# A two-layer MLP behind a short convolution: two more of the second layer's Strassen products split once more

## The chip, the cores and the metric

The kernel runs on one core of a Trainium2 chip. The metric is the time of one execution on the device in microseconds (us), as the median of several runs.

## The reference

`x` is (8, 4096, 192), 32,768 tokens of 192 values. A causal convolution over 7 tokens weighs each channel by a softmax over its head's 7 taps; the result goes through an MLP, 192 to 2048 with a hardswish gate and back to 192. All is float32.

```python
w = softmax(weight, axis=-1)                          # (8 heads, 7 taps)
y = np.einsum('hk,bskhg->bshg', w, x_unf)             # x_unf: 7 shifted views of padded x
h = y.reshape(32768, 192) @ w_in                      # 192 -> 2048
g = h * np.clip(h + 3.0, 0.0, 6.0) / 6.0
out = g @ w_out                                       # 2048 -> 192
```

## The kernel before, in words

The tokens are cut into 32 blocks of 1024 (`TB`), each two groups of N = 512. The two groups lie on the two halves of the 128 partitions, so a copy with the halves swapped (`swap_parts`) serves the other group. Block 0 has a path of its own (`out_direct`) that runs while weights are prepared. Blocks 1 to 31 run `first_layer` and then `second_layer`. All is under `tc.manual_schedule()`: each engine executes its instructions in the order in which the code issues them, and a block's first and second layers follow each other on TensorE.

**First layer.** y and w_in are split into three parts each (HIGH, LOW, MIX), and each of 16 steps n runs 18 matmuls (L508) into one PSUM slot of two banks. ACT multiplies the slot by 4097 between the parts (L520) and makes the relu (L302); VectorE makes the gate (L306), which writes g and releases the slot. Four slots rotate. Steps 0 to 7 give the quarters A11 and A22 of g, steps 8 to 15 give A21 and A12. Beside these steps GpSimd forms small sums of A11 (L578) and the sum S3 = A11 - A21 (L412, `g_sums`), and starts DMAs that add A22 onto A21 in place (L557, S1 = A21 + A22). The last two pairs of S1 are added by VectorE (L559). The convolution of a later block (L919, L921) is placed between as `jobs`.

**Second layer.** The contraction over 2048 with 192 outputs is a 2x2 matrix product by Strassen, with seven products P1 to P7 (`prod`), each over eight chunks of 128, 512 tokens wide and 96 output rows. The rows are three quarters of 32, and TensorE runs four column streams side by side, stream j writing rows 32j to 32j+31 of a PSUM bank. A plain step is a matmul of 512 columns; `put` counts it as 2 units, a small one of 256 columns as 1. Streams 0 to 2 run the three quarters of P4, P7, P2, P6 and P3. Stream 3 runs the first two quarters of P1 and of P5 by Strassen once more (`level_two`, seven small products of four 256-column matmuls), and their third quarter as plain steps: 82 units on each stream.

The small products need small weights (`w_s`, formed once, L587) and small sums of their operand: `s1` (of A11, on GpSimd) and `s5` (of S1, in A22's place, on VectorE, L578). Their results are passed between places in PSUM by ACT copies (L695 to L701) and VectorE adds (L456).

The order around the change is set by hand. `put` and `do` collect closures with a time in units, `do(t, ...)` at t - 0.5, and `second_layer` sorts all of them by time and runs them; that gives every engine's queue. `between` brings in the next block's split of y (L474, L937, L477), the swap, the load of x and some taps of the convolution. PSUM slots come from `free_slots`: the slots of gates 12, 13 and 14 become the banks d, e; b, x_; a, c. Two final sums and stores (`finish`) are left over and run as `jobs[-1]` of the next block's first layer. In the last block `ends`, `end_lower` and `end_upper` store in pieces.

Of the kernel before, what the change touches and what calls it, by code (L numbers as in the profile page):

```python
# [25 lines left out]
def kernel(  # L26
# [93 lines left out]
    w_s = cst.tile([P, 2, 4, NP // 2, QS], F32, name="w_s")  # L120
# [245 lines left out]

    new_results()
# [34 lines left out]
    def g_sums(engine, which, slots, width):  # L402

        forms = {
            3: (S3, A11, A21, ALU.subtract),
            2: (S2, S1, A11, ALU.subtract), 4: (S3, A12, S2, ALU.subtract),
        }
        for n in which:
            o, a, b, op = forms[n]
            for p in slots[::width]:  # L410
                r = slice(p, p + width)
                engine.tensor_tensor(out=o[:, r], in0=a[:, r], in1=b[:, r], op=op)  # L412
# [75 lines left out]
    y_own, y_other, pools, s1 = [], [None], [], []  # L488

    def swap_parts():  # L490
        y_other[0] = pools[0].tile([P, 3, K3, N], F32, name="y_other", tag="other")
        for n in range(3):
            swap(y_other[0][:, n], y_own[n])


    def first_layer(i, jobs):
# [6 lines left out]
        def mms(n, part, start=False, stop=False):  # L503
            group, c = divmod(n, NP)
            for s in range(K3):
                for k in range(2):
                    r = slice(k * D2, (k + 1) * D2)
                    nc.tensor.matmul(  # L508
                        out=psum[:, 2 * slots[n] + k], lhsT=r32(w_in_parts[part][r, c, s]),
                        rhs=r32(y_other[0][r, part, s] if group else y_own[part][r, s]),  # L510
                        start=start and s == 0, stop=stop and s == K3 - 1,
                        skip_group_check=True,
                    )
# [27 lines left out]
        for n in range(count):  # L541
# [7 lines left out]
            if n == 1:  # L549
                s1.append(ot.tile([P, NP, N], F32, name="s1", tag="shared")[:])  # L550
            if n < NP and n % 2:
                small_sums(s1[-1], A11, (1, 2, 3, 4), nc.gpsimd, every[n - 1 : n + 1])
            if n > NP and n % 2:
                pair = slice(n - NP - 1, n - NP + 1)
                g_sums(nc.gpsimd if n + 1 < count else nc.vector, (3,), range(NP)[pair], 2)
                if n + 3 < count:
                    nc.gpsimd.dma_start(out=S1[:, pair], in_=A22[:, pair], accum_op=ALU.add)  # L557
        for pair in (slice(NP - 2, NP), slice(NP - 4, NP - 2)):
            add(S1[:, pair], A21[:, pair], A22[:, pair])  # L559
# [20 lines left out]
    def small_weights(to, w):  # L580

        b11, b12, b21, b22 = (
            w_out[:, c::2, w, q * QS : (q + 1) * QS] for c in range(2) for q in range(2)
        )
        t1, t2, t3, t4 = (to[:, n] for n in range(4))
        for o, p, q in ((t1, b12, b11), (t2, b22, t1), (t3, b22, b12), (t4, b21, t2)):
            nc.gpsimd.tensor_tensor(out=o, in0=p, in1=q, op=ALU.subtract)  # L587

    def second_layer(i, between):
# [3 lines left out]
        ends = [psum[:, 2 * free_slots[0] + k] for k in range(2)] if last else [b, b]  # L593
        s5 = A22
        copy = nc.scalar.copy
        m = slice(0, DH)
        lo, hi = halves
        both = nc.sync, nc.scalar
        B, C, V = (bank[rows(3)] for bank in (x_, d, b))
        A, E = e[rows(3)], a[rows(3)]  # L600
        first, second, third, fourth = (rows(q) for q in range(4))
        late = {}
# [17 lines left out]
        def plain(j, bank, n, q, chunks, start=False):  # L620
            x, w = prod[n]
            x = S3 if x is None else x
            for k, ch in enumerate(chunks):
                put(j, 2, lambda ch=ch, k=k: matmul(
                    j, bank[rows(j)], w_out[:, ch, w, q * QS : (q + 1) * QS], x[:, ch],
                    start and k == 0,
                ))

        def small(n, m_, out, start=False):

            x, w = prod[n]
            sums, ws = (s1[-1], w_s[:, 0]) if n == 1 else (s5, w_s[:, 1])
            x11, x12, x21, x22 = four_parts(x)
            z1, z2, z3, z4 = four_parts(sums)
            b11, b12, b21, b22 = (
                w_out[:, h::2, w, q * QS : (q + 1) * QS] for h in range(2) for q in range(2)
            )
            t1, t2, t3, t4 = (ws[:, k] for k in range(4))
            xm, wm = {
                1: (x11, b11), 2: (x12, b21), 3: (z4, b22), 4: (x22, t4),  # L640
                5: (z1, t1), 6: (z2, t2), 7: (z3, t3),
            }[m_]
            for u in range(NP // 2):
                put(3, 1, lambda u=u: matmul(
                    3, out[:, lo], wm[:, u], xm[:, u], start and u == 0
                ))

        def plain_by_halves(j, n, q, t):
            w = prod[n][1]
            for ch in every:  # L650
                put(j, 1, lambda ch=ch: matmul(
                    j, ends[t][rows(j), halves[t]], w_out[:, ch, w, q * QS : (q + 1) * QS],
                    S3[:, ch, halves[t]], ch == 0,
                ))

        def tiles():
            new_results()
            if last:
                xts.insert(0, NP - 1)
            late.update(zip(("p7", "p5", "u3"), (results[0][m, n] for n in range(3))))  # L660

        for q in range(NQ):
            plain(q, d, 4, q, every, True)
            before = (1, 6, NP)[q]
            plain(q, c, 7, q, every[:before], True)
            plain(q, e, 1, 2, range(5 + q, 6 + q))
            do(clock[q], copy, out=e[rows(q + 1)] if q < 2 else p1[third], in_=e[rows(q)])
            plain(q, c, 7, q, every[before:])
            plain(q, a, 2, q, every[:6], True)
            plain(q, b, 6, q, every)  # L670
            plain(q, a, 2, q, every[6:])
            if last:
                plain_by_halves(q, 3, q, 0)
                plain_by_halves(q, 3, q, 1)
            else:
                plain(q, b, 3, q, every)

        def level_two(n, p, chunks, order):
            chunks, first_fill = list(chunks), [True]
            left = [list(chunks) for _ in halves]  # L680

            def fill_half(t, k):
                for _ in range(k):
                    ch = left[t].pop(0)
                    x, w = prod[n]
                    put(3, 1, lambda ch=ch: matmul(
                        3, (ends[0], x_)[t][fourth, halves[t]], w_out[:, ch, w, 2 * QS : 3 * QS],
                        x[:, ch, halves[t]], ch == 0,
                    ))

            def fill(k):
                plain(3, b, n, 2, [chunks.pop(0) for _ in range(k)], first_fill.pop() if first_fill else False)

            steps = {
                1: lambda: copy(out=B[:, lo], in_=A[:, lo]),  # L695
                2: lambda: copy(out=p()[first, lo], in_=A[:, lo]),
                6: lambda: copy(out=C[:, lo], in_=B[:, lo]),
                5: lambda: copy(out=p()[second, lo], in_=E[:, lo]),
                7: lambda: add(p()[second, hi], C[:, lo], p()[second, lo]),
                3: lambda: add(p()[second, lo], B[:, lo], p()[second, lo]),  # L700
                4: lambda: copy(out=p()[first, hi], in_=C[:, lo]),  # L701
            }
            to = {1: A, 2: A, 6: B, 5: E, 7: C, 3: B, 4: C}
            for step in order.split():
                if step[0] == "x":
                    fill(int(step[1]))
                elif step[0] in "lh":
                    fill_half("lh".index(step[0]), int(step[1]))
                else:
                    k = int(step)  # L710
                    small(n, k, to[k], k in (1, 5))
                    do(clock[3], steps[k])

        level_two(1, lambda: p1, range(5), "1 x5 6 5 2 7 3 4")
        do(14, copy, out=e[first], in_=V)
        level_two(
            5, lambda: late["p5"], range(NP),
            "1 l4 2 6 5 7 3 l2 4 l2 h8" if last else "1 x2 2 6 5 7 3 x1 4 x5",
        )

        for t, job in between:
            do(t, job)
        for t, n in ((16.2, 1), (16.2, 2), (30.5, 3), (34.5, 4)):
            do(t, small_sums, s5, S1, (n,), nc.vector)
        do(32, tiles)
        do(34, lambda: copy(out=late["p7"], in_=c[m]))
        do(38, copy, out=b[m], in_=p1[:])
        do(38, g_sums, nc.vector, (2,), every, 4)
        do(38, g_sums, nc.vector, (4,), every, 4)
        do(62, lambda: add(late["u3"], b[m], late["p7"]))  # L730
        do(62, lambda: add(late["p7"], late["u3"], d[m]))
        do(62, lambda: store(i, late["p7"], 1, 0))
        do(66, add, p1[:], a[m], p1[:])
        do(66, lambda: store(i, p1, 0, 0))

        def finish(k):
            p5, u3 = late["p5"], late["u3"]
# [6 lines left out]
        def end_lower():  # L744
            p5, u3, c12 = late["p5"], late["u3"], results[0][m, 6]
            two = slice(0, 2 * QS)
# [272 lines left out]
```

## Time and profile before

| what | value |
|---|---|
| median of 3 runs (lowest, highest) | 2226.74 us (2226.70, 2226.88) |
| span of the profiled execution | 2224.9 us |
| TensorE matmul busy | 2218.0 us |
| VectorE (DVE) busy | 1894.3 us |
| ScalarE (ACT) busy | 1379.2 us |
| GpSimd (POOL) busy | 823.8 us |
| one block in mid-run: first layer, second layer | 32.90 us, 35.47 us |

The profile is of one execution, whose span is 1.8 us shorter than the median of the runs. In its rows, `L615 PE MATMUL psum<-g,w_out 128*32 128x512 f32 x5440` is line 615, engine, operation, what it writes and reads, the tile and how often it runs; behind the bar stand the busy time and the mean duration in ns, and behind the second bar the engine's idle time just before, with what ended it. PEld is TensorE's weight load, which runs beside its matmuls. "POOLq" and "SPq" are the queues of the engines that issue DMAs. A timeline row begins with its start and its duration in us.

### The profile page before, as it was taken

To read this page: it belongs to the slowest core of one execution; us is meant where nothing else is said; L and a number is where in the kernel's file an instruction comes from. 1 tells how busy PE (TensorE), PEld (TensorE's weight loads), DVE (VectorE), ACT (ScalarE), POOL (GpSimd) and SP (SyncE) were. 2 spreads that over 40 slices of the span, in tenths; PEclk is the share of its full clock that TensorE was granted. 3 is DMA by queue.
4 is the path that set the end of the run, shared out by engine and by line. 5 is a ranking of instruction groups with operands and counts; after the bars stand their busy time and mean duration, and the time that the engine had idled before them with its cause. 6 is when DMAs were issued, how large, how long until landed. Compare 5 with 4: busy or idle time off the path is not lost.

```text
span 2224.9 us, 50339 instructions
## 1 busy us (share of the span) xinstructions
PE 2218.0 (100%) x21496; PEld 1532.7 (69%) x21496; DVE 1894.3 (85%) x1673; ACT 1379.2 (62%) x1678; POOL 823.8 (37%) x690
## 2 busy tenths in 40 slices
PE   9999999999999999999999999999999999999999
PEld 5467776677766777766777667776677776677766
DVE  8888888888888888888888888888888888888876
ACT  7457665576655676555766557665567655576654
POOL 2344432344422444223443234442244422344323
PEclk9999999999999999999999999999999999999999
DMA  6244224443244342344422444324434234442232
GB/s 157 57 98 85 49 58 91 85 83 62 53 82 91 77 80 47 71 91 84 85 48 58 91 87 81 67 49 82 91 79 81 47 67 91 84 84 52 55 77 34
DMA packets 253584, 166.57 MB, mean 75 GB/s; under 512 B 208017, under 2 KB 213137, under 8 KB 253361
## 3 DMA queue, kind: packets, MB, share of 16 engines
q1 hardware_dynamic: 234872, 129.46, 28.4%
q0 software_dynamic: 17248, 33.64, 8.7%
q8 instruction: 168, 2.75, 0.5%
q14 instruction: 56, 0.45, 0.1%
q10 hardware_dynamic: 1240, 0.27, 0.1%
HBM read 31.72 MB, written 25.17 MB: 26 GB/s over the span
## 4 chain that ended last, share of the span: by engine, by line
PE 99%; DVE 0%; DMA 0%; ACTq 0%; issue 0%; DVEq 0%; ACT 0%
PE psum L615 49%; PE psum L508 46%; PE psum L296 2%; PE psum L341 2%; DMA x<-in_x_dram 0%; DVE y L255 0%; DVE top L175 0%; ACTq L89 0%; PE psum L816 0%; DVE results L456 0%; DVE scale L171 0%; DVE y L251 0%; DVE scale L192 0%; DVEq L1014 0%; DVE results L462 0%
## 5 line engine op out<-in xcount | busy, mean ns | idle before, releaser
L615 PE MATMUL psum<-g,w_out 128*32 128x512 f32 (+1 forms) x6712 | 967.5, 552 | 0.0
L306 DVE SCALAR_TENSOR_TENSOR g<-g,psum 128x1024 f32<-128x1024 f32 (+1 forms) x528 | 618.3, 1186 | 198.8 <-ACT g L302 194.5
L578 POOL TENSOR_TENSOR s<-g 128x256 f32<-128x256 f32 x248 | 273.6, 1103 | 1241.1 <-DVE g L306 1200.5
L302 ACT ACTIVATE g<-psum,half 128x1024 f32<-128x1024 f32 (+1 forms) x528 | 564.8, 1087 | 6.0 <-PE psum L508 5.2
L615 PEld LDWEIGHTS psum<-g,w_out 128*32 128x32 f32 x6712 | 371.8, 110 | 246.0 <-issue 126.7
L508 PE MATMUL psum<-y,w_in 64*128 64x512 f32 x4464 | 521.4, 388 | 0.0
L508 PE MATMUL psum<-y_other,w_in 64*128 64x512 f32 x4464 | 516.0, 386 | 0.0
L520 ACT ACTIVATE psum<-psum 128x1024 f32<-128x1024 f32 x465 | 469.0, 1008 | 50.7 <-PE psum L508 48.4
L508 PEld LDWEIGHTS psum<-y,w_in 64*128 64x128 f32 x4464 | 413.5, 184 | 115.7 <-issue 26.0
L508 PEld LDWEIGHTS psum<-y_other,w_in 64*128 64x128 f32 x4464 | 418.1, 184 | 87.8
L615 PE MATMUL psum<-s,w_out 128*32 128x512 f32 (+1 forms) x3272 | 465.5, 570 | 0.0
L921 DVE SCALAR_TENSOR_TENSOR y<-x,c_sb,y 128x1536 f32<-128x1536 f32 x186 | 335.2, 1802 | 2.6 <-ACT y L919 1.3
L412 POOL TENSOR_TENSOR s<-g 128x1024 f32<-128x1024 f32 x93 | 285.9, 3074 | 26.2 <-DVE g L306 26.2
L615 PE MATMUL psum<-g,w_s 128*32 128x256 f32 x1240 | 282.8, 379 | 0.0
L615 PEld LDWEIGHTS psum<-s,w_out 128*32 128x32 f32 x3272 | 154.3, 110 | 81.9 <-issue 49.4
L615 PEld LDWEIGHTS psum<-g,w_s 128*32 128x32 f32 x1240 | 136.4, 110 | 67.7
L412 DVE TENSOR_TENSOR s<-g 128x2048 f32<-128x2048 f32 (+1 forms) x93 | 181.3, 1977 | 1.1
L615 PE MATMUL psum<-s,w_s 128*32 128x256 f32 x744 | 170.7, 379 | 0.0
L578 DVE TENSOR_TENSOR g<-g 128x1024 f32<-128x1024 f32 x124 | 151.7, 1224 | 5.3
L412 DVE TENSOR_TENSOR g<-g 128x2048 f32<-128x2048 f32 x62 | 139.1, 2284 | 0.0
L612 ACT COPY psum<-psum 32x512 f32<-32x512 f32 x93 | 51.3, 551 | 135.4 <-PE psum L615 135.4
L456 DVE TENSOR_TENSOR results<-psum,results 32x256 f32<-32x256 f32 (+3 forms) x128 | 69.3, 541 | 50.9 <-issue 45.5
(91 smaller groups left out, 1299.5 us busy)
## 6 DMA issues: line engine op xcount, KB each, us to landing
y_other<-y SPq DMA_DIRECT2D x186, 384.0 KB, 5.1
g<-g POOLq DMA_DIRECT2D x62, 512.0 KB, 5.0
out_dram<-results SPq DMA_DIRECT2D x378, 64.0 KB, 2.0
x<-in_x_dram SPq DMA_DIRECT2D x53, 388.5 KB, 7.7
stage<-in_moe_w_in_dram SPq DMA_DIRECT2D x16, 192.0 KB, 4.5
stage<-in_moe_w_out_dram SPq DMA_DIRECT2D x8, 384.0 KB, 6.8
x<-in_x_dram SPq DMA_DIRECT2D x7, 384.0 KB, 8.4
x<-in_x_dram POOLq DMA_DIRECT2D x2, 388.5 KB, 5.4
```

What stands on the lines that cost most here:

```text
L296: nc.tensor.matmul(out=psum[:, b], lhsT=w[r], rhs=src, start=start, stop=stop, skip_group_check=onto,)
L302: nc.scalar.activation(r6, h, ACT.Relu, bias=half[:], scale=1.0 / 6.0)
L306: nc.vector.scalar_tensor_tensor(out=g_, in0=g_, scalar=1.0, in1=h, op0=ALU.min, op1=ALU.mult)
L341: lambda p=p: nc.tensor.matmul(out=bank[j * QS : (j + 1) * QS, tokens], lhsT=w_out[:, p, w, cols], rhs=x[:, p, tokens], start=(first and p ...
L412: engine.tensor_tensor(out=o[:, r], in0=a[:, r], in1=b[:, r], op=op)
L456: nc.vector.tensor_tensor(out=out, in0=x, in1=y, op=op)
L508: nc.tensor.matmul(out=psum[:, 2 * slots[n] + k], lhsT=r32(w_in_parts[part][r, c, s]), rhs=r32(y_other[0][r, part, s] if group else y_own[ ...
L520: nc.scalar.mul(both(n), both(n), 4097.0)
L578: engine.tensor_tensor(out=o, in0=p, in1=q, op=op)
L612: streams[3].append((t - 0.5, lambda: fn(*args, **kw)))
L615: nc.tensor.matmul(out=out, lhsT=w, rhs=x, start=start, stop=True, tile_position=(0, j * QS), skip_group_check=True,)
L921: jobs.append(lambda k=k: nc.vector.scalar_tensor_tensor(out=y[:], in0=x[:, :, k : k + N], scalar=c_sb[:, k : k + 1], in1=y[:], op0=ALU.mu ...
```

## The change

P4 and P7 too go by Strassen once more, as P1 and P5 do, and the streams are laid out anew: 80 units each.

- Stream 0: P2's first quarter, the third quarters of P1 and P5, then P6 and P3. Stream 1: P2's second quarter, the seven small products of P4 with one of P5's in a place of its own (`aside`), P6, P3. Stream 2: P2's third quarter, the third quarters of P4 and P7, P6, P3. Stream 3: the small products of P1, P7 and P5.
- The sums for P4 (of A22) are formed by DMA: four copies on SyncE's queue after step 7 of the first layer (`copy_for_sums`), then four adding DMAs from GpSimd's queue behind steps 9, 11 and 13 (`add_for_sums`), into y's own region (`sums4`).
- S1 is formed wholly by adding DMAs, four in place of two and two VectorE adds. S3's sum for n = 13 moves from GpSimd to VectorE.
- The sums for P7 (of S3) are formed on VectorE in the region of `y_other` (`sums7`); those for P5 (of S1) by four ACT multiplies by 1 or -1 and four adding DMAs (`sums_by_dma`).
- P4's sums have the other sign (`PLUS`), so one quarter of its weights is negated once by ACT, and its steps negate and subtract.
- Split of y, swap and load of x move later in the second layer; results lie in A22; the last block loses its own tail.

The core of the diff:

```diff
         for n in range(count):
...
             if n < NP and n % 2:
-                small_sums(s1[-1], A11, (1, 2, 3, 4), nc.gpsimd, every[n - 1 : n + 1])
+                small_sums(sums[1], A11, (1, 2, 3, 4), nc.gpsimd, every[n - 1 : n + 1])
+            if n == NP - 1:
+                sums[4] = sums_in("own", "sums4")
+                copy_for_sums(sums[4], A22)
             if n > NP and n % 2:
                 pair = slice(n - NP - 1, n - NP + 1)
-                g_sums(nc.gpsimd if n + 1 < count else nc.vector, (3,), range(NP)[pair], 2)
-                if n + 3 < count:
-                    nc.gpsimd.dma_start(out=S1[:, pair], in_=A22[:, pair], accum_op=ALU.add)
-        for pair in (slice(NP - 2, NP), slice(NP - 4, NP - 2)):
-            add(S1[:, pair], A21[:, pair], A22[:, pair])
+                early = n + 3 < count
+                if n in ADD_AHEAD:
+                    add_for_sums(sums[4], A22, ADD_AHEAD[n])
+                g_sums(nc.gpsimd if early else nc.vector, (3,), range(NP)[pair], 2)
+                nc.gpsimd.dma_start(out=S1[:, pair], in_=A22[:, pair], accum_op=ALU.add)
+                if n in ADD_BEHIND:
+                    add_for_sums(sums[4], A22, ADD_BEHIND[n])
+
+    ADD_AHEAD = {NP + 1: (1,), NP + 3: (2,)}
+    ADD_BEHIND = {NP + 3: (3,), NP + 5: (4,)}
...
+    def copy_for_sums(to, x):
+        x11, x12, x21, x22 = four_parts(x)
+        s1, s2, s3, s4 = four_parts(to)
+        for o, p in ((s1, x22), (s2, x11), (s3, x11), (s4, x12)):
+            nc.sync.dma_start(out=o, in_=p)
+
+    def add_for_sums(to, x, which):
...
+        forms = {1: (s1, x21), 2: (s2, s1), 3: (s3, x21), 4: (s4, s2)}
+        for n in which:
+            o, p = forms[n]
+            nc.gpsimd.dma_start(out=o, in_=p, accum_op=ALU.add)
+
+    def sums_by_dma(to, x, n):
...
+        o, p, scale, q = {
+            1: (s1, x22, 1.0, x21), 2: (s2, x11, -1.0, s1),
+            3: (s3, x21, -1.0, x11), 4: (s4, s2, -1.0, x12),
+        }[n]
+        nc.scalar.mul(o, p, scale)
+        nc.gpsimd.dma_start(out=o, in_=q, accum_op=ALU.add)
...
+    def small_weights(n):
+        b11, b12, b21, b22 = w_quarters(n)
+        t1, t2, t3, t4 = w_smalls(n)
+        third = (t3, b12, b22) if n == PLUS else (t3, b22, b12)
+        for o, p, q in (third, (t1, b12, b11), (t2, b22, t1), (t4, b21, t2)):
             nc.gpsimd.tensor_tensor(out=o, in0=p, in1=q, op=ALU.subtract)
+        if n == PLUS:
+            nc.scalar.mul(b22, b22, -1.0)
...
+        s3_places = e[fourth, lo], a[fourth, lo], x_[fourth, lo], d[fourth, lo]
+        s1_places = e[second, lo], c[second, lo], x_[second, lo], x_[second, hi]
+        aside = c[second, hi]
+        places = {1: s3_places, 4: s1_places, 5: s3_places, 7: s3_places}
+        onto = {1: b, 4: d, 5: p5, 7: p7}
...
+        def step(n, k):
+            A, E, B, C = places[n]
+            p, plus = onto[n], n == PLUS
+            op = ALU.subtract if plus else ALU.add
+            if k == 1:
+                (negated if plus else copy)(out=B, in_=A)
+            elif k == 2:
+                copy(out=p[first, lo], in_=A)
+            elif k == 6:
+                copy(out=C, in_=B)
+            elif k == 5:
+                (negated if plus else copy)(out=stash(n), in_=E)
+            elif k == 7:
+                add(p[second, hi], C, stash(n), op)
+            elif k == 3 and plus:
+                add(p[second, lo], stash(n), B, op)
+            elif k == 3:
+                add(p[second, lo], B, stash(n))
+            else:
+                copy(out=p[first, hi], in_=C)
...
         for q in range(NQ):
-            plain(q, d, 4, q, every, True)
...
+            plain(q, a, 2, q, True)
+        plain(0, e, 1, 2, True)
+        do(clock[0], copy, out=b[third], in_=e[first])
+        plain(0, x_, 5, 2, True)
+        do(clock[0] + 1, copy, out=p5[third], in_=x_[first])
+        for k in (1, 5, 6, 2, 7, 3):
+            small(1, 4, k)
+            do(clock[1], step, 4, k)
+        small(1, 5, 4, aside)
+        small(1, 4, 4)
+        do(clock[1], step, 4, 4)
+        do(clock[1] + 1, copy, out=p5[first, hi], in_=aside)
+        plain(2, d, 4, 2, True)
+        plain(2, c, 7, 2, True)
+        do(clock[2] + 1, copy, out=p7[third], in_=c[third])
+        for q in range(NQ):
+            plain(q, b, 6, q)
+            plain(q, b, 3, q)
+
+        waiting = {(7, 5): 48.5, (7, 2): 48.6, (7, 7): 49}
+        for n, k in (
+            [(1, k) for k in (1, 5, 6, 2, 7, 3)] + [(7, 1), (1, 4)]
+            + [(7, k) for k in (5, 6, 2, 7, 3)] + [(5, 1), (7, 4)]
+            + [(5, k) for k in (5, 6, 2, 7, 3)]
+        ):
+            small(3, n, k)
+            do(waiting.get((n, k), clock[3]), step, n, k)
+        do(clock[3] - 4 + 0.2, lambda: add(p5[first, hi], places[5][3], p5[first, hi]))
...
+        do(0.6, sums7)
+        do(21, lambda: small_sums(sums[7], S3, (4,), nc.vector))
+        for t, n in ((30, 1), (33, 3), (37, 2), (58, 4)):
+            do(t, sums5, n)
+        do(32.4, lambda: copy(out=spare["own"][m], in_=b[m]))
+        do(32.6, lambda: add(a[m], a[m], spare["own"][m]))
+        do(33, g_sums, nc.vector, (2,), every[: NP // 2], 4)
+        do(37, g_sums, nc.vector, (2,), every[NP // 2 :], 4)
+        do(50, g_sums, nc.vector, (4,), every[: NP // 2], 4)
+        do(53, g_sums, nc.vector, (4,), every[NP // 2 :], 4)
         for t, job in between:
             do(t, job)
...
+        do(57, lambda: store(i, a, 0, 0))
+        do(64.2, lambda: add(u3, b[m], p7))
+        do(64.3, lambda: add(p7, u3, d[m]))
+        do(64.4, lambda: store(i, p7, 1, 0))
...
             if i + 1 < NB:
-                between = [(13, split_high), (15, split_rest), (18, swap_parts)]
+                between += [(40.4, split_high), (41, split_low), (49.5, split_mix), (53, swap_parts)]
```

In the changed file the first layer's matmul is line 522, its gate 307, its multiply 534, the second layer's matmul 670, S1's adding DMA 574, the adding DMAs of P4's sums 614, of P5's sums 625 with their ACT multiply 624, the negation of weights 646, and `step` 720 to 734.

## The prediction

> **What bounds the kernel now.** I began with the page's busy shares, then its chain that ended last.
>
> ```profile
> PE 2218.0 (100%) x21496; PEld 1532.7 (69%) x21496; DVE 1894.3 (85%) x1673; ACT 1379.2 (62%) x1678; POOL 823.8 (37%) x690
> ...
> PE 99%; DVE 0%; DMA 0%; ACTq 0%; issue 0%; DVEq 0%; ACT 0%
> ```
>
> TensorE is never idle, and 99% of the chain is its own work, so only less matmul or a new wait of TensorE can change the time. The chain in order of time gives a block:
>
> ```profile
> 1057.14 32.90 PE psum L508 x288
> 1090.05 35.47 PE psum L615 x216
> ```
>
> A block is 32.90 us of first layer and 35.47 of second, 68.37 together, and 31 blocks follow. The second layer is 82 units (256 columns on each of the four streams). In the timeline the sets of stream matmuls start at 1096.44, 1096.87 and 1097.30: a unit is 0.43 us (35.47 / 82 = 0.433).
>
> Third, how a hand-over from TensorE to another engine and back looks:
>
> ```profile
> 1097.33 0.59 PE L615 MATMUL psum<-s,w_s 128*32 128x256 f32 x2
> ...
> 1097.99 0.34 ACT L697 COPY psum<-psum 32x256 f32<-32x256 f32 x1 [1.10 <-PE psum L615]
> ...
> 1098.78 0.55 ACT L612 COPY psum<-psum 32x512 f32<-32x512 f32 x1 [0.45 <-PE psum L615]
> ...
> 1099.38 0.11 PEld L615 LDWEIGHTS psum<-g,w_out 128*32 128x32 f32 x1 [0.21 <-ACT psum L612]
> ...
> 1099.49 0.59 PE L615 MATMUL psum<-g,w_out 128*32 128x256 f32 x2
> ```
>
> The set begun at 1097.33 is done a unit later, 1097.76, and ACT starts at 1097.99: 0.2 us. The L612 copy ends at 1099.33 and the weight load that waited for it runs at 1099.38: 0.05, then 0.11 for the load. So a hand-over costs 0.2 + the operation + 0.16. This load belongs to stream 3's row quarter, and the copy touches another quarter of the same PSUM bank: the program waits by bank. Such waits exist 62 times:
>
> ```profile
> PEld psum L615 <- ACT psum L612: 13.8, 62, 0.2
> ```
>
> They cost TensorE nothing: two units (0.86 us) lie between the producer matmul and the waiting one, and the hand-over takes about that.
>
> **What the change removes.** Two units of 82: 0.86 us a block, 26.6 in 31. Before's 2226.7 less that is 2200.
>
> **What it adds.** Every wait of TensorE in the changed second layer follows from its instruction order and semaphores, and many now have *no* unit between the producer and the waiter. Positions are units from the second layer's start; the steps (product, small product) are those of the code.
>
> *a) The boundary, unit 0.* P2 now comes first, in bank a, which is the PSUM slot that gate 14 of the first layer reads. Before, P4's bank d came first, free two gates earlier.
>
> ```profile
> 1089.94 3.48 DVE L306 SCALAR_TENSOR_TENSOR g<-g,psum 128x1024 f32<-128x1024 f32 x3 [1.17 <-ACT g L302]
> 1089.97 6.64 PE L615 MATMUL psum<-g,w_out 128*32 128x512 f32 x63
> 1093.45 1.71 DVE L412 TENSOR_TENSOR s<-g 128x1024 f32<-128x1024 f32 x1
> ```
>
> Those are gates 13 to 15, 1.16 us apart: gate 13 ends at 1091.10. The change also moves S3's sum for n = 13 from GpSimd into VectorE's queue just behind gate 13. So 1091.10 + 1.37 (row below) + gate 14's 1.22 + 0.16 = 1093.85 against 1089.97: **3.9 us**.
>
> *b) Hand-overs without slack.* With the copy's 0.34 to 0.37 and the add's 0.43, one costs 0.7 (ACT) or 0.8 (VectorE). They stand at units 8 (copy of (1,5)), 16 ((1,2)), 20 ((4,1) and (1,7)), 24 ((1,3) add), 28 (two copies in a row, 1.05) and 48 ((4,4)): 0.72 + 0.72 + 0.82 + 0.85 + 1.05 + 0.7 = **4.9 us**. Each stops all streams, because TensorE's queue is in order.
>
> *c) Unit 33.* The matmul of (7,5) in bank a waits for VectorE's a += P1, behind four ACT copies that follow unit 32 (0.55, 0.36, 0.36, 0.58): 0.2 + 1.85 + 0.2 + 0.69 (96x512 add) less the unit between, 0.43: **2.5 us**.
>
> *d) Units 36 and 40.* (4,7) and (4,3), VectorE adds that now release bank x_, stand behind the halves of S2's sum.
>
> ```profile
> L412 DVE TENSOR_TENSOR g<-g 128x2048 f32<-128x2048 f32 x62 | 139.1, 2284 | 0.0
> ...
> L412 DVE TENSOR_TENSOR s<-g 128x1024 f32<-128x1024 f32 x31 | 42.3, 1365 | 1.1
> ```
>
> From VectorE's free moment in c): at 36, 2.28 + 0.43 + 0.16 less 3 units = **1.5**; at 40, 2.28 + 0.43 + an ACT copy's 0.35 less 4 units = **1.3**.
>
> *e) Unit 49.* Three more ACT copies (0.37, 0.37, 0.58) less a unit: **0.9**.
>
> *f) Unit 60.* The matmul of (5,5) in bank a waits for a's transpose, behind (7,7) 0.43, the split 1.75, S4's first half 2.28, (7,3) 0.43, the second half 2.28, the transpose 0.71: 7.9 us, beside which 11 units (4.7) and e)'s stall (0.9) pass: **2.2**.
>
> *g) Unit 64.* u3 must read b before P3 is added to it: 0.69, **0.7**.
>
> Sum 3.9 + 4.9 + 2.5 + 1.5 + 1.3 + 0.9 + 2.2 + 0.7 = 17.9, less 0.86: 17.0 a block, 528 in 31.
>
> *Costed at nothing.* VectorE's adds for S3's small sums (4 x 1.22) replace S1's small sums; GpSimd's A11 sums (L578) end at +24 us, ahead of unit 4. ACT gains four 1.0-us operations (L624) in a second layer where it idles half the time; without that cover, c) grows by 1.0 each.
>
> *DMA.* A block's adding DMAs go from 2 to 12, all in GpSimd's queue, and SyncE gets four copies of 512 KB.
>
> ```profile
> g<-g POOLq DMA_DIRECT2D x62, 512.0 KB, 5.0
> ...
> q0 software_dynamic: 17248, 33.64, 8.7%
> q1 hardware_dynamic: 234872, 129.46, 28.4%
> ```
>
> 8.7% of the span over 62 accumulations bounds one at 3.1 us of all 16 engines: 12 cost up to 37 us. With the 20 that queue 1 takes in a block now (28.4% of 2224.9, over 31), and four copies (2 us each by the rate of the swaps, six of 384 KB in about 10 us), the engines would be busy some 66 of 85 us. Early use has slack: the first needed lands before unit 20. The new accumulations move rows of 1 KB, before's 2 KB, which no row shows. Bounds: same price per byte (nothing added); twice as long (12 x 3.1 more than a block holds: the sum S1 late by 5 to 10 us). I take the same price, nearest to this row; the upper end widens the range. Issues occupy GpSimd:
>
> ```profile
> L557 POOL DMA_DIRECT2D g<-g x62 | 74.5, 1201 | 19.9 <-POOL s L412 19.9
> ```
>
> Ten more are 12 us, on an engine with 60% idle: cost nothing.
>
> *Once.* In the first block ACT's negation of B22 waits for seven weight sums of GpSimd and holds the convolution's first multiply and L520 behind it.
>
> ```profile
> L587 POOL TENSOR_TENSOR w_s<-w_out 128x128 f32<-128x128 f32 x4 | 5.4, 1342 | 1.0 <-DVE w_out L212 1.0
> ```
>
> From 94.9: 7 x 1.34 = 9.4, + 0.5 + 1.6, so 106.4 against 101.5, and VectorE behind it: between 5 and 8, I take 7. The last block loses its split tail (an add, transpose and store later): 0 to 4, I take 2.
>
> The profiled execution: 2224.9 + 528 + 7 + 2 = 2761.9; around the span lie 1.8 us (median 2226.7): **2764**.
>
> **Two rules weighed.** The Trainium skill, "PSUM — Partial Sum Buffer", section "PSUM bank collisions raise a hardware error", says that two engines may touch one bank at once if they are in different quarters of 32 rows. The 0.2-us waits above show this program waiting across quarters nevertheless; by the rule only a) and g) are needed, and a program guarded so would take 2200 + 31 x 4.6 + 9 = 2352 (estimate). "TensorE: Matmul & The Clock Gate", Part 1, speaks against the change: an idle window of about 3.4 us halves the clock for as long. No idle gap lies in before's trace (clock digits 9 throughout), so none here shows it; with a) in each block it would add about 1.7 x 31 = 53 (estimate).
>
> **Rivals.**
> 1. *DMA late.* If 1-KB rows cost 1.5 times, or the queue backs up, ACT's L624 (which waits for all four S1 sums and stands ahead of c)) starts 4 to 8 us late: 31 x 4 to 8 over the forecast, 2890 to 3010. For it: slack at unit 28 of about 1 us. Against: 5.0 us to landing.
> 2. *Shorter stalls.* If ACT's and VectorE's hand-overs run partly inside the drain of the other streams, b) to f) fall by a third: 13.3 / 3 x 31 = 137 less, 2627. For it: the free 0.2-us waits.
> 3. *Faster.* The waits cost nothing as the 62 do now: it holds only if every wait lies within TensorE's buffered work, decides where stalls sum below 0.86 us a block, and gives 2200 + 9 = 2209. Against: buffered work shown covers 0.2 us; a) alone is 3.9.
> 4. *The units aren't saved*: streams of 256 columns load weights twice as often, 6 x 0.11 = 0.66 in 0.86 us; before 5. It would add 26.6: 2791. Against: the loads still fit.
>
> **Chances.** Forecast's band, 2690 to 2850, with rival 4 inside: 70%. Rival 1: 14%. Rival 2: 12%. Rival 3: 4%. The range takes in half of rivals 1 and 2: 2620 to 2940. A change under 0.2% can't be told from none in this measurement; faster by more 0.03, same 0.01, slower 0.96.
>
> **What would show it.** TensorE's busy share falls to about 80%; the first second-layer matmul waits 3 to 4 us for VectorE L307; VectorE and ACT enter the chain with about a fifth of it; the matmul work itself shrinks by 0.86 us a block. Waits of TensorE on DMA would mean rival 1; a share above 95% would make the prediction wrong.

## The result, and the profile after

The changed kernel takes 2997.65 us (median of 4 runs, 2989.08 to 3003.57) against 2226.81: 1.346 times as long, 95% interval [1.344, 1.348]. The profiled execution has a span of 2994.9 us. A block takes 93.2 us where it took 68.4: 24.8 more, and 31 times that is the whole difference of 770 us in span.

The page of the changed kernel, busy times first and then the queues:

```profile
PE 2458.3 (82%) x22920; PEld 1565.5 (52%) x22920; DVE 2002.7 (67%) x1791; ACT 1553.0 (52%) x2018; POOL 1101.0 (37%) x972
...
q0 software_dynamic: 164992, 196.12, 42.9%
q1 hardware_dynamic: 301880, 194.68, 27.3%
...
sums<-g POOLq DMA_DIRECT2D x155, 512.0 KB, 7.7
...
g<-g POOLq DMA_DIRECT2D x124, 512.0 KB, 8.5
```

TensorE is idle for 18% of the span; before it was never idle. The adding DMAs of queue 0 take 42.9% of the 16 engines' time, 8.7% before, and one needs 6.1 to 8.5 us from issue to landing (medians of the page, by what it writes and reads), 5.0 before. Both dynamic queues together are 2102 us of DMA work, 68 us of a 93-us block (26.6 before).

Who held TensorE, from the view of the waits (us in total, times, longest):

```profile
PEld psum L670 <- DVE g L307: 191.3, 31, 7.2
...
PE psum L670 <- DVE g L307: 178.2, 31, 6.7
...
PEld psum L670 <- DVE psum L462: 151.5, 93, 2.4
...
PEld psum L670 <- DMA sums<-g: 94.8, 30, 3.9
...
PEld psum L670 <- DVE g L468: 77.0, 31, 2.5
```

In each of the 31 blocks the second layer's first weight load waits 6.2 us for gate 14 (L307), and the matmuls stand idle for 5.75. Three times a block an add (L462) holds TensorE, once the transpose of a (L468), once a DMA into the small sums. The forecast had all but the last.

Where in the second layer the time goes can be read to the unit: stream 3 starts one small matmul per unit, so a start that comes later than 0.4287 us after the one before is a stall or a slow unit. The table gives the means over 31 blocks in us a block, for the forecast, the changed kernel, and some of the experiments below. The row of unit 0 has an ordinary step of 0.6 in it (all that is left of it in e2, e7, e9 and e11), and in the changed kernel 0.4 of slow clock as well (e4, at full clock, has 6.4 there).

| units | held by | forecast | changed | e2 | e3 | e5 | e7 | e9 | e11 |
|---|---|---|---|---|---|---|---|---|---|
| 0 | gate 14 (a) | 3.9 | 6.8 | 0.6 | 6.8 | 6.8 | 0.6 | 0.6 | 0.6 |
| 2 to 6 | matmuls at half clock | 0 | 1.8 | 0 | 1.3 | 2.1 | 0 | 0 | 0 |
| 8 to 28 | hand-overs (b) | 4.2 | 4.3 | 5.8 | 4.3 | 1.5 | 5.8 | 0.9 | 0 |
| 32, 34 | a += P1 (c) | 2.5 | 2.2 | 7.0 | 2.2 | 0.1 | 2.2 | 0.1 | 0 |
| 36 to 44 | VectorE, DMA (d) | 2.8 | 3.1 | 3.1 | 3.1 | 8.6 | 3.1 | 4.4 | 0.5 |
| 48 to 52 | ACT copies (b, e) | 1.6 | 1.3 | 1.3 | 1.3 | 1.3 | 1.8 | 0.4 | 0.7 |
| 60, 62 | transpose of a (f) | 2.2 | 2.2 | 2.2 | 2.2 | 0 | 2.2 | 0.1 | 0.2 |
| 64 to 70 | u3 (g) | 0.7 | 0.5 | 0.5 | 0.5 | 1.4 | 1.4 | 4.1 | 3.6 |
| 76, 78 | P5's fourth small sum | 0 | 3.3 | 2.9 | 0 | 5.2 | 0.1 | 2.4 | 0 |
| block | | 85.4 | 93.2 | 90.9 | 88.8 | 95.1 | 84.2 | 80.7 | 72.8 |

Steps b) to g) come to 14.0 in the forecast and 13.6 measured. What the forecast lacks stands in three rows: unit 0, the half clock behind it, and unit 76. The boundary, in the timeline of the changed kernel:

```profile
1434.02 1.22 DVE L307 SCALAR_TENSOR_TENSOR g<-g,psum 128x1024 f32<-128x1024 f32 x1 [1.16 <-ACT g L303]
1434.46 1.29 POOL L614 DMA_DIRECT2D sums<-sums  x1 [3.05 <-DMA sums<-g]
1435.26 2.86 POOL L418 TENSOR_TENSOR s<-g 128x1024 f32<-128x1024 f32 x1
1435.28 3.94 DVE L418 TENSOR_TENSOR s<-g 128x1024 f32<-128x1024 f32 x1
...
1439.14 2.34 DVE L307 SCALAR_TENSOR_TENSOR g<-g,psum 128x1024 f32<-128x1024 f32 x2
...
1440.40 4.41 PE L670 MATMUL psum<-g,w_out 128*32 128x512 f32 x23 [6.27 <-DVE g L307]
```

The moved sum L418 takes 3.94 us on VectorE, not 1.37: it starts with GpSimd's own L418 (the sum for n = 11) and ends 1.1 us after it, about what it takes alone. Over the 31 blocks it takes 2.26 to 4.40 us, 3.41 on average. GpSimd's is that late because its queue stood 3.05 us at L614, P4's second adding DMA, which waits for the first to land. Then 23 matmul records take 4.41 us, where 24 took 2.36 in the kernel before. The same stretch cut by time (window, its length, busy time and count of PE, PEld, DVE, ACT and POOL, granted clock, DMA share, GB/s) shows why:

```profile
1440.40:1443.80 3.40, 3.40 (x20) 1.50 (x24) 3.26 (x3) 0.00 (x0) 3.40 (x4) 0.50 1.10 173
1443.80:1447.20 3.40, 2.84 (x33) 1.29 (x29) 2.63 (x3) 0.71 (x2) 0.91 (x1) 0.88 1.17 169
1447.20:1460.00 12.80, 10.99 (x129) 5.66 (x125) 3.92 (x4) 3.15 (x7) 0.00 (x0) 1.00 0.73 121
```

The clock is 0.50 for the first 3.4 us. Over the run it is granted at half for 262 us, in pieces of 3.4, 6.8 and 10.2 us; before, for 4.7 us at the start. And unit 76:

```profile
1386.63 1.06 ACT L624 ACTIVATE sums<-sums 128x1024 f32<-128x1024 f32 x1
1387.98 1.28 POOL L625 DMA_DIRECT2D sums<-g  x1 [12.30 <-ACT g L734]
1388.01 1.58 SPq L267 DMA_DIRECT2D y_other<-y_own  x1
...
1399.31 0.40 PE L670 MATMUL psum<-sums,w_out 128*32 128x256 f32 x1 [1.87 <-DMA sums<-g]
```

P5's fourth small sum is issued at 1388.0, together with the last two swap DMAs of the next block's y, and TensorE's matmul that needs it starts 11.3 us later.

### The profile page after: what moved, and what is told of

Read it like the earlier page. It is cut to its first block, busy times and chain, and to the rows that moved or that the text cites. A ratio compares the mean times of both kernels' runs of the same rounds, so it can differ in the third digit from the quotient of the medians.

```text
span 2994.9 us, 55245 instructions
## 1 busy us (share of the span) xinstructions
PE 2458.3 (82%) x22920; PEld 1565.5 (52%) x22920; DVE 2002.7 (67%) x1791; ACT 1553.0 (52%) x2018; POOL 1101.0 (37%) x972
## 3 DMA queue, kind: packets, MB, share of 16 engines
q0 software_dynamic: 164992, 196.12, 42.9%
## 5 line engine op out<-in xcount | busy, mean ns | idle before, releaser
L670 PE MATMUL psum<-g,w_out 128*32 128x512 f32 (+1 forms) x7440 | 1244.8, 594 | 326.7 <-DVE g L307 178.2
L307 DVE SCALAR_TENSOR_TENSOR g<-g,psum 128x1024 f32<-128x1024 f32 (+1 forms) x528 | 621.8, 1186 | 203.2 <-ACT g L303 202.7
L670 PE MATMUL psum<-sums,w_out 128*32 128x256 f32 x1984 | 466.2, 404 | 199.0 <-DMA sums<-g 67.5
L522 PE MATMUL psum<-y_own,w_in 64*128 64x512 f32 x4464 | 528.4, 392 | 0.2 <-DVE results L403 0.2
L598 POOL TENSOR_TENSOR sums<-g 128x256 f32<-128x256 f32 x248 | 273.3, 1102 | 677.2 <-DVE g L307 676.5
L522 PEld LDWEIGHTS psum<-y_own,w_in 64*128 64x128 f32 x4464 | 429.5, 186 | 99.5 <-issue 18.7
L670 PE MATMUL psum<-sums,w_s 128*32 128x256 f32 x1984 | 477.4, 381 | 0.0
L670 PEld LDWEIGHTS psum<-sums,w_out 128*32 128x32 f32 x1984 | 203.2, 116 | 413.6 <-DMA sums<-g 94.8
L462 DVE TENSOR_TENSOR psum<-psum,sums 32x256 f32<-32x256 f32 (+1 forms) x124 | 62.0, 500 | 383.3 <-PE psum L670 230.0
L462 DVE TENSOR_TENSOR g<-psum,g 32x256 f32<-32x256 f32 (+1 forms) x217 | 108.7, 501 | 306.5 <-PE psum L670 218.9
L670 PE MATMUL psum<-s,w_out 128*32 128x256 f32 (+1 forms) x992 | 294.6, 489 | 0.0
L418 DVE TENSOR_TENSOR g<-g 128x2048 f32<-128x2048 f32 x124 | 283.5, 2287 | 2.0
L670 PEld LDWEIGHTS psum<-sums,w_s 128*32 128x32 f32 x1984 | 202.8, 109 | 84.9 <-DVE psum L462 26.6
L574 POOL DMA_DIRECT2D g<-g x124 | 195.9, 1580 | 18.4 <-POOL s L418 18.4
```

Source lines behind the costliest of these rows:

```text
L307: nc.vector.scalar_tensor_tensor(out=g_, in0=g_, scalar=1.0, in1=h, op0=ALU.min, op1=ALU.mult)
L462: nc.vector.tensor_tensor(out=out, in0=x, in1=y, op=op)
L522: nc.tensor.matmul(out=psum[:, 2 * slots[n] + k], lhsT=r32(w_in_parts[part][r, c, s]), rhs=r32((y_other if group else y_own)[0][r, part, s ...
L598: engine.tensor_tensor(out=o, in0=p, in1=q, op=op)
L670: nc.tensor.matmul(out=out, lhsT=w, rhs=x, start=start, stop=True, tile_position=(0, j * QS), skip_group_check=True,)
```

## The experiments

Theory A was: the excess over the forecast is these three things (VectorE's sum beside GpSimd's, the clock after idleness, the sum that lands beside the swap), and the rest are the waits by bank without slack of the forecast. Each run has one edit to the changed kernel unless it says otherwise; times are medians, beside 2226.8 for the kernel before and 2997.65 for the changed one.

**e1, S3's sum behind the gates.**

```diff
-                g_sums(nc.gpsimd if early else nc.vector, (3,), range(NP)[pair], 2)
+                if early:
+                    g_sums(nc.gpsimd, (3,), range(NP)[pair], 2)
+                elif n + 1 == count:
+                    g_sums(nc.vector, (3,), every[NP - 4 :], 2)
```

> Only S3's sum for n = 13 moves, from between gates 13 and 14 on VectorE to behind gate 15. Theory A (the 6.2-us boundary stall is the sum ahead of gate 14, 1.4 us of its own and 2.6 of standing beside GpSimd's L418): gate 14 ends about 2.4 us after the first layer's matmuls instead of 6.3, TensorE is idle under 3 us, the clock stays up and the slow first units (1.8 us) go too: 5.5 us a block less, about 170 in all, 2830. Rival B (the boundary waits for something else, such as the late second half of ACT's relu, or the sum moves the same stall to a later unit): under 60 us less. In between, 2880: the wait goes but the slow units stay, so they have another cause than the idle gap.

Measured 3157.38 us, ratio 1.419 [1.416, 1.421]. The edit was badly made: the DMA that adds A22 onto A21 for n = 13 stayed where it was and so came first, and the sum read S1 in place of A21 and had to wait for that landing. Unit 0 fell to 3.0 as theory A has it, but VectorE's queue stood, and unit 20 waited 9.4 us. It says nothing on the total; e6 repeats it properly.

**e2, other names for the banks.**

```diff
-        d, e, b, x_, a, c = (psum[:, 2 * n + k] for n in ours for k in range(2))
+        a, e, b, x_, d, c = (psum[:, 2 * n + k] for n in ours for k in range(2))
```

> Only the names of the banks change: a and e take the slot of gate 12, d and c that of gate 14, so the first matmul of the second layer waits for gate 12. Theory A: the stall at unit 0 goes wholly (6.2 us), the slow units go (1.8), and P2's last two chunks, which gates 14 and 15 write, now wait at units 12 and 14, about 1 us together: 7 us a block less, 217 in all, 2780. Rival B (the second layer can't start before gate 14 whatever the bank): unchanged within 20.

Measured 2921.58, ratio 1.313 [1.310, 1.315]: 76 us less, not 217. The boundary and its slow units went as expected (8.0 us a block, table), so they are the bank's wait for gate 14. But 6.3 of it came back at units 12 to 34. The waits of e2:

```profile
DVE psum L462 <- ACT sums L778: 282.8, 31, 10.6
...
ACT sums L624 <- DMA g<-g: 160.9, 31, 6.6
```

ACT now stands 5.2 us a block at L624 until S1's last adding DMA has landed; the copies behind it, and VectorE's a += P1 behind those (L778), keep TensorE. Of this wait the changed kernel has none: its late boundary had covered it. This is the forecast's first rival, in the place that it named, but not in the changed kernel.

**e3, the swap later.**

```diff
-                between += [(40.4, split_high), (41, split_low), (49.5, split_mix), (53, swap_parts)]
+                between += [(40.4, split_high), (41, split_low), (49.5, split_mix), (78, swap_parts)]
```

> Only the six swap DMAs of the next block's y move, from unit 53 to unit 78. Theory A (at unit 76 TensorE waits for P5's fourth small sum because its adding DMA shares the 16 DMA engines with the swap: 11 us from issue to landing instead of 6): it lands some 4 us earlier, the 2.8-us wait at unit 76 goes, with 0.5 us of slow clock behind it: 3 us a block, about 95 in all, 2900. Rival B (the sum is late because its ACT multiply stands behind VectorE's queue and is issued late): landing and wait stay, within 25 of 2998. Rival C (the swap then arrives late for the next first layer): a new wait of y_other there, and slower than 2998.

Measured 2863.85, ratio 1.287 [1.284, 1.289]: 134 us less. The wait at unit 76 is gone (3.3 to 0), with part of the half clock of the next boundary. The adding DMA of P5's fourth sum now lands 6.3 us after its issue (median), where it took 11.6 in the changed kernel. The next first layer waits no longer for y_other than there (about 1 us in the whole run): from its first matmul's start to its last's it takes 32.7 us, 32.9 in the changed kernel and 32.6 in the kernel before. Theory A, and more than its 95.

**e4, work in place of idleness.**

```diff
+        for _ in range(7):
+            matmul(2, d[third], w_out[:, 0, T4, 2 * QS : 3 * QS], A11[:, 0], True)
         for q in range(NQ):
             plain(q, a, 2, q, True)
```

> Adds work and removes no wait: seven matmuls of 512 columns, whose result is overwritten, ahead of the second layer's first matmul, so that TensorE works for about 6.0 us of the 6.2 it otherwise waits at the boundary. Theory A (the first units run at half speed because TensorE was idle): the boundary stays as long, units 0 to 7 run at 0.43 us each, 1.8 us a block less, 55 in all, 2943, and the granted clock of the span rises to about 0.98. Rival B (the slow first units have another cause, such as weight loads or operands that arrive late): 2998 or up to 20 more.

Measured 2932.14, ratio 1.318 [1.314, 1.322]: 65 us less with more work. The timeline cut by time, of e4, beside that of the changed kernel above (the boundary, then the first units):

```profile
1423.80:1430.20 6.40, 6.40 (x23) 1.75 (x25) 6.25 (x4) 2.09 (x3) 6.10 (x5) 1.00 0.94 145
1430.20:1433.60 3.40, 3.38 (x39) 1.66 (x31) 3.23 (x4) 0.34 (x1) 3.40 (x4) 1.00 1.11 171
```

The boundary is as long (6.4 at unit 0), units 2 to 6 are no longer slow, and half clock falls from 262 to 82 us. So the slow units come from the idle gap and not from loads or operands.

**e5, banks apart.**

```diff
+        f, h = (psum[:, 2 * free_slots[0] + k] for k in range(2))
-        s3_places = e[fourth, lo], a[fourth, lo], x_[fourth, lo], d[fourth, lo]
-        s1_places = e[second, lo], c[second, lo], x_[second, lo], x_[second, hi]
+        s3_places = e[fourth, lo], h[fourth, lo], x_[fourth, lo], d[fourth, lo]
+        s1_places = f[second, lo], c[second, lo], x_[second, lo], x_[second, hi]
...
-        plain(0, e, 1, 2, True)
+        plain(0, f, 1, 2, True)
```

> Only places change: the fourth PSUM slot takes the plain third quarter of P1, P4's place A, and the place E of stream 3, so that copies and matmuls of different quarters no longer meet in banks a and e. Theory A (the stalls at units 8, 16, 28, 33 and 60, 6.9 us a block as measured in the changed kernel, are waits by bank between different quarters and not for data): they go, some 2 us of unit 33's coming back at unit 36 because VectorE is no earlier: 4.7 to 6.9 a block less, 2785 to 2850. Rival B (they are waits for data or for engines that are late anyway): under 40 us less. Rival C (the first sum S1 by DMA becomes the bound, as it did when the bank names were changed): half of the gain or less, about 2900.

Measured 3052.08, ratio 1.371 [1.368, 1.373]: 54 us slower, which no theory had. The five waits did go (7.1 us in the table's rows), so they were by bank and not for data. But unit 36 still waits for VectorE's S2 sum and the add behind it, which start no earlier; there the short stalls have become one long one:

```profile
1593.31 1.06 PE L671 MATMUL psum<-g,w_out 128*32 128x512 f32 x1 [3.74 <-DVE psum L462]
```

After it the clock falls to half, in 29 of the 31 blocks, and over the run it is at half for 601 us against 262 (mean granted clock 0.902 against 0.957).

**e6, S3's sum behind the gates with its DMA.**

```diff
+                elif n + 1 == count:
+                    for p in (slice(NP - 4, NP - 2), pair):
+                        g_sums(nc.vector, (3,), range(NP)[p], 2)
+                        nc.gpsimd.dma_start(out=S1[:, p], in_=A22[:, p], accum_op=ALU.add)
```

> S3's sum for n = 13 behind gate 15 on VectorE, and the DMA that adds onto the same rows behind it (in the run before, the DMA went first, so that the sum waited for its landing and read S1). Theory A: the boundary falls to the 3.0 us that the run before showed at unit 0, the slow units to almost nothing, as there; the sums S1 of n = 13 land about 3 us later, with no cost at units 20 to 24: 5.3 us a block less, 2830. Rival B (VectorE's sums of S3 for P7, or S1 now late, take the time back at units 24 to 44): 2900 or more.

Measured 2912.55, ratio 1.308 [1.306, 1.310]: 85 less, rival B. Unit 0 is 3.1 and the slow units 0.5, 5.0 us a block less, as expected; units 32 and 34 rise from 2.2 to 5.1, where ACT's L624 waits 3.3 us a block for S1, as in e2.

**e7, P5's sums later, with e2's and e3's edits.**

```diff
-        for t, n in ((30, 1), (33, 3), (37, 2), (58, 4)):
+        for t, n in ((40, 1), (42, 3), (46, 2), (58, 4)):
```

> Renamed banks and the late swap together, and ACT's multiplies for P5's sums placed about ten units later (40, 42, 46 for 30, 33, 37). Theory A (with the boundary gone, ACT's queue stands at the first of these multiplies until S1's last adding DMA has landed, and the copies behind it hold TensorE at units 32 to 34 for 4.8 us more): that goes, so 90.9 - 3.5 (swap) - 4.8 = 82.6 us a block, 2660. Rival B (S1 itself lands too late for the matmuls of P5's third quarter from unit 32 on): TensorE waits there for a DMA instead, about 2780. Rival C (P5's small sums then land late at unit 60): a wait there, 2700 to 2780.

Measured 2723.31, ratio 1.223 [1.221, 1.225]. Units 32 and 34 are back at 2.2: the 4.8 us were ACT's queue and not S1 itself. The clock is 0.999, with no half-clock piece after the start. A block is 84.2 and not 82.6: unit 64 grew by 0.9 and units 48 to 52 by 0.5, and the swap's row fell by 2.8 and not by 3.5.

**e8, no tight waits.** All four slots, places by bank so that 4 units lie between a matmul and each copy or add of its bank, some steps placed later, the swap at 78.

```diff
-        d, e, b, x_, a, c = (psum[:, 2 * n + k] for n in ours for k in range(2))
+        a, G_, X, H1, H2, d, F, b = (psum[:, 2 * n + k] for n in ours for k in range(2))
...
+        s3_places = G_[fourth, lo], X[fourth, lo], H1[fourth, lo], H2[fourth, lo]
+        s1_places = H2[second, lo], X[second, lo], G_[second, lo], H1[second, lo]
+        aside = X[second, hi]
...
+            do(clock[1] + (4 if k in (7, 3) else 0), step, 4, k)
...
+        for t, n in ((37, 1), (41, 3), (44, 2), (58, 4)):
...
+    ADD_AHEAD = {NP + 1: (1,)}
+    ADD_BEHIND = {NP + 3: (3, 2), NP + 5: (4,)}
```

> All four PSUM slots are used and the places, two of P4's adds, its last copy and the second half of S2's sum are put so that at least 4 units lie between a matmul and the copy or add of the same bank, except for u3 at unit 64 (0.5 us); P4's second adding DMA goes behind the third, the swap late. Theory A (all stalls of the changed kernel were waits without slack, the boundary, the idle clock and the late sum): 67.5 + 0.5 + about 2 for DMA waits, 70 us a block, 2280. Rival B (transfers: the DMA engines work 66 us a block in the changed kernel, which no longer fits beside 68): TensorE waits for DMA at units 20 to 44 or 60 to 76, 74 to 78 us a block, 2400 to 2530, DMA share over 85%. Rival C (VectorE, 64 us busy a block): TensorE waits on VectorE, the same range. It is not expected to beat the kernel before.

Measured 2677.12, ratio 1.202 [1.200, 1.204], slower than any of the three. All of b) and c) is gone, and in its place stand other waits: P4's sums at units 24 (2.1) and 36 (3.3), and u3 at 64 (5.3). The two dynamic queues' share is 79%, under rival B's 85. The waits of e8:

```profile
POOL sums L614 <- DMA sums<-sums: 240.2, 31, 9.2
...
PEld psum L670 <- DVE g L462: 157.6, 31, 5.9
```

P4's fourth adding DMA needs the second, which in the new order landed late, and GpSimd's queue stood 7.7 us a block before it. So the wait at unit 24 was made by this run's own order; it is gone in e9.

**e9, P5's fourth sum later**, on e8, with P4's DMAs in the change's order again.

```diff
-        for t, n in ((37, 1), (41, 3), (44, 2), (58, 4)):
+        for t, n in ((37, 1), (41, 3), (44, 2), (66, 4)):
```

> From the run without tight waits: P4's adding DMAs in the order of the change again, and ACT's multiply for P5's fourth small sum at unit 66 in place of 58. Theory A (P5's second and fourth sums are a chain of three DMAs, each 6 us and more from issue to landing, behind S1's own, and a shorter second layer leaves no time for it): the 5.3-us stall of u3 at unit 64, which came from ACT standing at that multiply, and the stalls at 24 to 36 shrink, and a new wait of TensorE for a DMA of 4 to 8 us stands at unit 76; about 80 us a block, 2590. Rival B (the stall at 64 is VectorE's own load): it stays at 64 and unit 76 has none, 2640 or more. Rival C (both go): 73 us a block, 2370.

Measured 2595.03, ratio 1.164 [1.163, 1.166], the fastest run that leaves nothing out. The stall at 64 falls only to 3.4 (4.1 with the units behind it), and a new one of 1.9 stands at 76, between theory A and rival B. What is left at 64 is rival B's, VectorE's own queue: u3's wait for it is 98.9 us in all in e9, 99.3 in e10 and 98.8 in e11. The timeline of e9 shows the chain to unit 76; ACT's multiply waits for a landing, the adding DMA for the multiply, and TensorE for the DMA:

```profile
1302.12 1.06 ACT L624 ACTIVATE sums<-sums 128x1024 f32<-128x1024 f32 x1 [1.26 <-DMA sums<-sums]
1303.47 1.28 POOL L625 DMA_DIRECT2D sums<-g  x1 [6.68 <-ACT sums L624]
1311.57 0.40 PE L670 MATMUL psum<-sums,w_out 128*32 128x256 f32 x1 [1.86 <-DMA sums<-g]
```

**e10 and e11, without the sums by DMA.** e10 is e9 without P5's four multiplies and adding DMAs, e11 also without P4's four copies and four adding DMAs.

```diff
-        for t, n in ((37, 1), (41, 3), (44, 2), (66, 4)):
-            do(t, sums5, n)
+        sums[5] = sums[1]
...
-                sums[4] = sums_in("own", "sums4")
-                copy_for_sums(sums[4], A22)
+                sums_in("own", "sums4")
+                sums[4] = sums[1]
```

> From the one before; leaves out P5's four small sums (four ACT multiplies and four adding DMAs; the small products read other rows instead). Theory A: the wait at unit 76 goes wholly, and P4's and S1's DMAs meet less traffic: 72 to 75 us a block, 2330 to 2430. Rival B (VectorE, 64 us busy in a block, is the bound by then): the time stays within 40 of the one before, with TensorE waiting on VectorE at 36 to 64.

> From the one before; leaves out P4's sums too (four copies and four adding DMAs; the small products read other rows instead). Theory A (what the kernel without tight waits still loses is all due to sums made by DMA): no wait on a DMA is left but for S1's, 68.5 to 70 us a block, 2230 to 2280. Rival B (VectorE and ACT queues hold TensorE still): 72 us a block or more, 2340 and up.

Measured 2495.35 (ratio 1.121 [1.119, 1.122]) and 2365.50 (1.062 [1.061, 1.064]): 3.8 and 4.1 us a block less. In e10 the wait at unit 76 goes wholly, as its theory A has it, and in e11 no DMA holds the second layer any more, but the time is rival B's. e10 misses 2430 because P4's sums still hold unit 36 (2.3). e11's page and waits:

```profile
PE 2268.1 (96%) x22920; PEld 1606.4 (68%) x22920; DVE 1927.6 (82%) x1791; ACT 1432.2 (61%) x1894; POOL 818.5 (35%) x724
```

```profile
PEld psum L666 <- DVE g L462: 98.8, 31, 3.3
```

What is left is mostly u3 behind VectorE's queue (3.6 a block). So even with P4's and P5's small sums left out the kernel is 6% slower than before. Without its stalls (5.0 in sum, unit 0's ordinary step left out) an e11 block would be 67.8, about the 67.5 that two units less make: the saving is real and is never reached.

**e12, P4's adding DMAs behind S1's.**

```diff
-    ADD_AHEAD = {NP + 1: (1,), NP + 3: (2,)}
-    ADD_BEHIND = {NP + 3: (3,), NP + 5: (4,)}
+    ADD_AHEAD = {NP + 1: (1,)}
+    ADD_BEHIND = {NP + 3: (3,), NP + 5: (2,), NP + 7: (4,)}
```

> The changed kernel with one difference: the second and fourth of P4's adding DMAs go behind S1's of steps 13 and 15 in GpSimd's queue, so that GpSimd no longer stands 3 us for the first one's landing ahead of S3's sum for n = 11. Theory A (VectorE's sum for n = 13 takes 3.9 us and not 1.2 because it stands beside GpSimd's sum for n = 11): GpSimd's sum ends 3 us earlier, VectorE's takes 1.2 to 1.4, and the boundary stall is 4.2 as forecast in place of 6.8; still over 3.4, so the slow units stay in part; P4's second sum lands later, a wait of up to 3 us at unit 24. 2920 to 3010. Rival B (VectorE's sum is slow for another reason): it still takes 3 us or more and the boundary stays at 6.8.

Measured 2911.94, ratio 1.308 [1.306, 1.310]. The timeline of e12:

```profile
1310.00 2.86 POOL L418 TENSOR_TENSOR s<-g 128x1024 f32<-128x1024 f32 x1
...
1314.31 1.22 DVE L418 TENSOR_TENSOR s<-g 128x1024 f32<-128x1024 f32 x1
1315.45 2.34 DVE L307 SCALAR_TENSOR_TENSOR g<-g,psum 128x1024 f32<-128x1024 f32 x2
...
1316.72 4.04 PE L670 MATMUL psum<-g,w_out 128*32 128x512 f32 x23 [3.56 <-DVE g L307]
```

GpSimd's sum is over before VectorE's begins, VectorE's takes 1.22, and TensorE waits 3.56: theory A, and step a) about as forecast. Unit 24 lost nothing, and the time is 8 us below the theory's range. Still the slow units stay, at 1.4.

## Why the prediction was wrong, point by point

The direction, the mechanism and most sizes held: b) to g) measured 13.6 for 14.0, and the two units are saved. The time missed the range by 58 us, 234 over the forecast. Three terms were wrong:

- **Step a)**, 3.9 for the boundary, was mis-sized: TensorE stands idle there for 5.75 us a block (178.2 in 31). It took 1.37 for the moved sum, the mean of a row whose sums meet GpSimd's for 0.2 us in most blocks; the one in the timeline shown took 1.71 and met it for 0.6, which was the warning. In the changed kernel the moved sum takes 3.41 on average, and in 29 of the 31 blocks that is 1.1 us more than the time for which it stands beside GpSimd's. e12 puts GpSimd's sum elsewhere and finds 1.22, and a wait of 3.56. The step lacked 1.9 us a block, 57 in all. The Trainium skill, "SBUF — State Buffer", section "SBUF: two separate sides", has the rule: of a VectorE instruction with two SBUF inputs and a GpSimd instruction that reads SBUF, the one that starts first holds a shared port pair to its end, and the other blocks. The 3.94 and the 1.22 agree with it; the gates, which read PSUM too, kept their 1.2 us.
- **The clock** was weighed but left out of the sum, since before's trace has no idle TensorE. It cost 2.2 us at the boundary (1.8 in units 2 to 6, 0.4 in unit 0's row) and about 0.6 behind unit 76, 87 in all; the estimate by the Trainium skill, "TensorE: Matmul & The Clock Gate", Part 1, had been 53. e4 shows the cause. The page asks for an idle window of about 3.4 us; here half clock followed shorter gaps too (last section).
- **"Costed at nothing", DMA.** The price of the transfers was right (66 us a block forecast, 68 measured; the adding ones 41 for 37), and the early uses were in time. The step failed because it looked at the first sums needed and not at the last: P5's fourth, at unit 76, shares the engines with the swap. 2.7 us a block, 84 in all; e3 removes it.

Together 228 of the 234. Smaller differences cancel: the first block lost 2.3 us and not 7 and the end is 2.5 shorter and not 2 longer (9 less), b) to g) are 12 less in 31 blocks, and about 0.8 us a block (26) is placed by no row of the table; the first layer's 32.9 for 32.6 is 0.3 of it.

Of the rivals, the first ("DMA late") gave a band that holds the result, 2890 to 3010, but that is luck: in the changed kernel ACT's L624 doesn't wait for S1 at all. It does as soon as the boundary is cut (e2, e6). Nor do the 1-KB rows cost 1.5 times (1.16, last section). So the sign that was named for it misleads: TensorE does wait for DMAs (94.8 us), but for P5's fourth small sum. The other signs: a busy share of 82% for 80, and 5.75 us of waiting for L307 for 3 to 4; the shares of the chain can't be read, because the page follows it back through 1% of the span only. The second was wrong: b) to f) measured 13.1 for 13.3, so next to nothing of them was hidden. The third fell with a) alone, the fourth with e11. What the page "PSUM — Partial Sum Buffer" says of different quarters of one bank no run here tests, as none leaves out a wait between quarters. e5 and e8 choose other places instead: the waits go, the time mostly doesn't.

The causes of what the forecast lacked are shown, each by a run (e12 and e2, e4, e3), and e5 shows that the forecast's waits at units 8, 16, 28, 33 and 60 are by bank. The rest of b) and steps d), e) and g) are read from the waits alone. What e9 still loses at units 36 to 44 is 2.5 us a block for P4's sums (TensorE's loads wait 77.4 us in 31 blocks for DMAs `sums<-sums`) and 1.2 for S1's (37.9 us for `g<-g`); with P4's sums left out (e11) neither wait is there. Not tested is another order of VectorE's work ahead of u3, where e9 to e11 still wait.

## What to carry to other kernels

Count the units between producer and waiter before counting units saved: two units less are worth 0.86 us a block, and one hand-over without slack costs nearly that. A stall that is removed ahead of a fixed later wait is not gained but moved there, and if it makes one idle gap long enough it brings a slower clock as well (e5). Sums formed by chained DMAs need the time of every landing in the chain, here 6 to 8 us each; find the last one's deadline, not the first one's.

## What the runs showed of the hardware that was not expected

- TensorE's clock fell to half after gaps shorter than the boundary's 6.3 us: of e11's 30 gaps of 2.8 us, 10 were followed by a half-clock piece, and 25 of e12's 31 gaps of 3.56 us. Each lasted 3.4 us or twice that, so a gap of 2.8 can cost another 1.7 (an estimate, half of 3.4).
- An adding DMA costs by bytes more than by rows: a row of 1 KB took 112 ns and one of 2 KB 193 ns in the changed kernel, so half as long rows made the transfer 1.16 times as long. A plain copy's row of 1 KB took 50 ns.
